# Reordering the loads and the first products of a fused spectral-mixer and MLP block, forward and backward

## The chip, the cores and the metric

The kernel runs on one core of a Trainium2 chip. The metric is the device time of one execution in microseconds (us). Five engines of a core appear below, each with its own in-order queue of instructions: TensorE (PE, matrix products; PEld is its loading of weights), VectorE (DVE), ScalarE (ACT), GpSimd (POOL) and SyncE (SP), which here does little but issue DMA transfers. "PEq", "SPq" and so on are the queues where an issue itself is recorded.

## The reference

The program computes a block and all of its gradients. S = 2048 tokens, D = 1024, F = 3584, bfloat16 in and out:

```python
mod = (silu(c) @ w_mod).reshape(1, 6, 1, -1)
sa, ca, ga, sb, cb, gb = mod rows 0..5
h = layernorm(x) * (1 + ca) + sa
x = x + ga * irfft2(rfft2(h) * (w_r + 1j * w_i))
h = layernorm(x) * (1 + cb) + sb
x = x + gb * (gelu(layernorm(h) @ w1 + b1) @ w2 + b2)
```

The outputs are x and, by `jax.vjp` with `grad_out`, the nine gradients for x, w_r, w_i, w1, b1, w2, b2, c and w_mod.

## The kernel before, in words

The Fourier transforms are products with tables of sines and cosines, after "folds" that use the symmetries of tokens and columns. The tokens lie in four chunks of 512; a chunk is loaded half in plain order by SP and half in turned order by indirect DMAs of POOL (`load_tok`, L142). F is worked in 28 blocks of 128 rows ("blocks" below).

The tile framework lays the instructions of each engine in an order by its own priorities, following the order of the code except where `issue_after` or `high_priority` says otherwise. What stands in an engine's queue runs in that order.

The stages that matter here, in the order of the program:

1. **Lead-in** (to about 60 us). The rows ca and gb of `mod` are made by `mod_block` (L273): for each half row eight products of silu(c) with a 128x8x512 block of w_mod (tile `wblk`, 1 MB, a ring of three slots), a cast, and for ca an addition of 1 on DVE. Chunks 0 and 1 of x get their layer norm: chunk 0 on DVE (`ln_dve`, L391), chunk 1 on ACT (`ln_act`, L376: four passes for sums, four for squares). `norm_act` (L417) applies the norm, DVE multiplies by the row 1 + ca. The gb row is turned into a column (tile `pc`, L434).
   grad_out comes in four quarters of 512 tokens (`load_go`, L350, 1 MB each). Each quarter is turned by 32 products with an identity or a reversing matrix (tile `pt`, L466); DVE (L470) and ACT (L474) evacuate the turned quarter and scale it by gb into `gBoT`. Then g·w2^T for the quarter and the first two blocks: sixteen products (`ph_part`, tile `pp`, L450). A block is 32 products; its four results are cast by DVE or ACT (L456), and POOL stores the block to `d_ph` in memory. w2^T comes through transposing DMAs on SP (`load_w2t`, L341; `wt` has four slots).
   POOL and DVE make indices for the sine tables, ACT the sines (L527). The sa row follows (L849), its first half and its second straight behind the last quarter.
2. **Blocks ahead of the spectral part.** `PH_EARLY = 8` (L868): blocks 0 to 7, and block 8 behind the loop, so nine of the 28 blocks lead. While PE works on them, DVE and ACT norm chunks 2 and 3 and fold the tokens.
3. **Spectral part** (from 120.18 us): `s_fwd` (tile `pu`, L573), the products with W, and the way back; its last products (tile `po`) end at 219.30 us. Behind it PE does the blocks that are left (L943); DVE and ACT at the same time consume the transform's output chunk by chunk (`consume_fwd`, L898): unfold, multiply by ga, add x, a layer norm (`ln_mix`, L401: half on DVE, half on ACT L410 and L413; `norm_act` L421), multiply and add cb and sb, a second norm. The normed chunk 0 is turned into `n3Ta` among the last blocks (L957).
4. **First MLP product.** A list by hand (`plan`, L1096) gives PE's order: z(0,0), the second halves of the four last blocks (64 products), z(0,1) to z(0,3), then first and second product in turn. z(b,g) is 32 products of token quarter b and four columns of w1 (L1006), evacuated by ACT (L1009) from two pools of two slots (`ps_s`, `ps_d`); the gelu and its derivative follow on ACT (L1013, L1017, L1019) and DVE. `bo` is the second product (L1060).

Behind that come the gradients. A third pool, `ps_f`, has four slots for the results of the blocks; before the change the turned quarters of grad_out use it too.

Of the kernel before, what the change touches and what calls it, by code (L numbers as in the profile page):

```python
# [10 lines left out]
FP32 = mybir.dt.float32  # L11
BF16 = mybir.dt.bfloat16
# [23 lines left out]
def kernel(  # L36
# [407 lines left out]
    def ph_part(fc, js, behind_=None):  # L444
        ph2 = phs[fc % 4]
        for j in js:
            pp = ps_f("pp")
            for cch in range(NDC):
                with tc.issue_after(behind_.ins) if behind_ else ExitStack():
                    last_pe[0] = nc.tensor.matmul(pp[:], lhsT=wt[:, fc % 4, cch, :], rhs=gBoT[j][:, cch, :],  # L450
                                                  start=(cch == 0), stop=(cch == NDC - 1))
            q = (0, 2, 3, 1)[j]
            ov = ph2[:, :, q * P:(q + 1) * P]
            pv = pp[:, :].rearrange("p (i w) -> p i w", w=P)
            with tc.high_priority():
                nc.any.tensor_copy(out=ov, in_=pv)  # L456
        if js[-1] == 3:
            nc.gpsimd.dma_start(out=d_ph[fc * P:(fc + 1) * P, :], in_=ph2.rearrange("p i w -> p (i w)"))

    for j in range(4):  # L460
        for cch in range(NDC):
            pt = ps_f("pt")
            for a in range(4):
                q = (0, 2, 3, 1)[a] if j % 2 == 0 else (1, 3, 2, 0)[a]
                with ordered() if last_pe[0] else ExitStack():
                    last_pt = nc.tensor.matmul(pt[:, q * P:(q + 1) * P], lhsT=gos[j][:, a, cch * P:(cch + 1) * P], rhs=(ident, irev)[a // 2],  # L466
                                               start=True, stop=True)
            if cch % 2 == 0:
                with tc.high_priority():
                    nc.vector.tensor_scalar(out=gBoT[j][:, cch, :], in0=pt[:], scalar1=gb_col[:, cch:cch + 1], scalar2=0.0,  # L470
                                            op0=ALU.mult, op1=ALU.add, accum_out=gu[:, j, cch:cch + 1])
            else:
                with tc.high_priority():
                    nc.scalar.activation(out=gBoT[j][:, cch, :], in_=pt[:], func=ACT.Identity, scale=gb_col[:, cch:cch + 1],  # L474
                                         accum_out=gu[:, j, cch:cch + 1])
        for fc in range(2):
            ph_part(fc, (j,), last_pt)

    gslot = [0]

    def gview(width, dt):
        o = gslot[0]
        gslot[0] += (2 * width + 15) // 16 * 16
        return genv[:, o:o + 2 * width].bitcast(dt)

    def iota(pattern, base, mult, width):
        ti = gview(width, I32)
        nc.gpsimd.iota(ti, pattern=pattern, base=base, channel_multiplier=mult)
        return ti

    def to_f(ti, width):
        tf = gview(width, FP32)
        nc.gpsimd.tensor_copy(out=tf, in_=ti)
        return tf

    def pts(out, in0, s1, s2, o0, o1=None):
        kw = {} if o1 is None else {"op1": o1}
        nc.gpsimd.tensor_scalar(out=out, in0=in0, scalar1=s1, scalar2=s2, op0=o0, **kw)

    kevi = iota([[1, 264]], 0, 0, 264)  # L500
    kevc = kevi.bitcast(FP32)
    nc.gpsimd.tensor_copy(out=kevc, in_=kevi)
    kev = gview(512, FP32)
    for r in range(2):
        pts(kev[:, r * 256:(r + 1) * 256], kevc[:, 0:256], 2.0, float(r), ALU.mult, ALU.add)
    kod = gview(512, FP32)
    for r, (mul, add) in enumerate(((2.0, 1.0), (-2.0, 1023.0), (2.0, 257.0), (-2.0, 767.0))):
        pts(kod[:, r * P:(r + 1) * P], kevc[:, 0:P], mul, add, ALU.mult, ALU.add)
    rown = to_f(iota([[256, 2]], 1, 2, 2), 2)
    rowr = to_f(iota([[-256, 2]], 1023, -2, 2), 2)  # L510
    rowo = [(rown, rowr)[r % 2][:, r // 2:r // 2 + 1] for r in range(4)]
    rowe = [rown[:, r:r + 1] for r in range(2)]
    jf, jod = kevc, kod.rearrange("p (s w) -> p s w", w=256)[:, :, 0:P]
    gidx = reg.tile([P, 2, 1024], I32, name="gidx", tag="px0")
    gcount, trig_in = [0], [None]

    def trig(dst, colv, rowv, nrow, width, modn, cosine):
        idx = gidx[:, gcount[0] % 2, :]
        gcount[0] += 1
        sh = float(3 * modn // 4 if cosine else modn // 2)  # L520
        for r in range(nrow):
            ov = idx[:, r * width:(r + 1) * width]
            pts(ov.rearrange("p (s w) -> p s w", s=2) if len(colv.shape) == 3 else ov, colv, rowv[r], sh, ALU.mult, ALU.add)
        n = nrow * width
        nc.vector.tensor_scalar(out=idx[:, 0:n], in0=idx[:, 0:n], scalar1=modn - 1, scalar2=None, op0=ALU.bitwise_and)
        with tc.issue_after(x_sqrt.ins):
            trig_in[0] = nc.scalar.activation(out=dst, in_=idx[:, 0:n].rearrange("p (r w) -> p r w", w=width), func=ACT.Sin,  # L527
                                 bias=negpi[:], scale=2 * np.pi / modn)
# [5 lines left out]
    def gen_mats():  # L534
        for cl, colv, modn in ((CE, kev, 2048), (SE, kev, 2048), (CO, kod, 4096), (SO, kod, 4096)):
            sm = (smA, smB)[cl % 2]
            rows, n = (rowo, 4) if cl % 2 else (rowe, 2)
            if cl == SE:
                nc.gpsimd.memset(kev[:, 0:1], 512.0)
            for r in range(0, n, 2):  # L540
                trig(sm[:, cl // 2, r:r + 2, :], colv, rows[r:r + 2], 2, 512, modn, cl < 2)
            if n == 2:
                nc.gpsimd.dma_start(out=d_SF[:, cl, 0:n], in_=sm[:, cl // 2])
        for cl, colv, modn in ((CE, jf[:, 0:256], 1024), (SE, jf[:, 1:257], 1024), (CO, jod, 2048), (SO, jod, 2048)):
            trig(em1[:, 0, 2 * cl:2 * cl + 2, :], colv, rowe, 2, 256, modn, cl < 2)
# [308 lines left out]
    gb2s = small.tile([P, NDC], FP32, tag="u_rt", bufs=1)  # L854
    nc.vector.reduce_sum(out=gb2s[:], in_=gu[:, 0:4, :].rearrange("p j c -> p c j"), axis=AX.X)
# [872 lines left out]
```

## Time and profile before

| | us |
|---|---|
| median of 3 runs | 1386.9 (1386.55 to 1392.74) |
| span of the profiled execution | 1385.4 |
| PE busy / DVE busy / ACT busy | 1357.9 / 1067.4 / 765.1 |
| first product of the spectral part | 120.18 |
| first product of z(0,0) / z(0,4) | 316.24 / 361.57 |

The profiled execution's span runs from its first to its last instruction; the median lies 1.5 us above it, which is taken as what lies around the span. In the rows quoted below a timeline gives the start, the duration, the engine, the line and operation, output and input, shapes, the count, and in brackets the idle time of the engine just ahead of it with what ended that. A row of a table by windows gives the busy time of PE, PEld, DVE, ACT and POOL (in brackets the instructions), then the granted clock of PE as a share of full speed, the busy share of the 16 DMA engines and GB/s.

### The profile page before, as it was taken

The page shows a single profiled execution, that of the slowest core. Times are in us where ns is not written, and L with a number is a line of the kernel's source. Part 1 is how long each engine was busy: PE and PEld are TensorE (multiplying, and loading weights), DVE is VectorE, ACT ScalarE, POOL GpSimd, SP SyncE. Part 2 cuts the span into 40 slices and gives each one's busy share as a digit, 9 for nine tenths or more (in the row PEclk, how much of TensorE's full clock was granted, in tenths as well). Part 3 has the DMA queues.
Part 4 walks back from the last instruction along what each step waited for, and adds up shares of the span by engine and source line. Part 5 has one row for each costly group of instructions (what it writes and reads, how often), then busy time and mean ns, then how long its engine had stood idle before and what let it go on. Part 6 is the DMA issues. An engine that isn't in the chain of part 4 may idle for free. (4 is left out here: it accounts for less than half of the span.)

```text
span 1385.4 us, 18669 instructions
## 1 busy us (share of the span) xinstructions
PE 1357.9 (98%) x6931; PEld 655.6 (47%) x6931; DVE 1067.4 (77%) x1477; ACT 765.1 (55%) x1084; POOL 357.4 (26%) x438
## 2 busy tenths in 40 slices
PE   5899999999999999999999999999999999999999
PEld 2445565444443444444444444444654555454444
DVE  5898889997988787887711488889888588968980
ACT  6855667658877765765413684446633464544311
POOL 5340633201112122122211011112344320332351
PEclk9999999999999999999999999999999999999999
DMA  9973665999787776697899779998779879899991
GB/s 329 279 243 88 166 173 179 258 272 362 252 258 228 223 253 223 205 279 252 256 309 220 210 187 275 293 294 243 205 217 264 223 150 263 214 252 244 308 329 52
DMA packets 356177, 330.08 MB, mean 238 GB/s; under 512 B 203834, under 2 KB 298448, under 8 KB 355958
## 3 DMA queue, kind: packets, MB, share of 16 engines
q1 hardware_dynamic: 313990, 200.76, 56.1%
q0 software_dynamic: 35328, 120.26, 25.5%
q10 hardware_dynamic: 6768, 7.87, 1.6%
q8 instruction: 54, 0.88, 0.3%
q14 instruction: 37, 0.30, 0.1%
HBM read 165.73 MB, written 114.87 MB: 203 GB/s over the span
## 5 line engine op out<-in xcount | busy, mean ns | idle before, releaser
L450 PE MATMUL pp<-gBoT,wt 128*128 128x512 bf16 x896 | 200.2, 381 | 0.5 <-DVE gBoT L470 0.3
L1160 PE MATMUL pg<-w1T,gzr 128*128 128x512 bf16 x896 | 196.0, 379 | 0.8 <-DMA gzr<-d_gz 0.8
L1596 PE MATMUL gw1acc<-gzh,n3n 128*128 128x512 bf16 x640 | 139.6, 379 | 0.0
L1006 PEld LDWEIGHTS <-w 128*128 128x128 bf16 x896 | 87.4, 98 | 108.5 <-issue 4.4
L1160 PEld LDWEIGHTS <-gzr 128*128 128x128 bf16 x896 | 86.5, 98 | 109.6 <-issue 5.9
L1596 PEld LDWEIGHTS <-n3n 128*128 128x128 bf16 x896 | 87.4, 98 | 105.2 <-issue 1.3
L450 PEld LDWEIGHTS <-wt 128*128 128x128 bf16 x896 | 87.6, 98 | 102.5 <-issue 3.1
L1006 PE MATMUL pz<-n3Tb,w 128*128 128x512 bf16 x448 | 100.1, 382 | 2.3 <-DVE w2sD L1082 2.3
L1006 PE MATMUL pz<-n3Ta,w 128*128 128x512 bf16 x448 | 98.7, 379 | 0.0
L1009 ACT ACTIVATE gt<-pz,b_col 128x512 bf16<-128x512 f32 x112 | 73.3, 683 | 41.0 <-PE pz L1006 40.6
L195 DVE TENSOR_TENSOR ct<-ct 128x2048 bf16<-128x2048 bf16 (+1 forms) x84 | 91.5, 1118 | 5.1 <-ACT n L421 2.5
L1600 ACT CAST gwo<-gw1acc 128x512 bf16<-128x512 f32 x56 | 32.3, 582 | 111.5 <-PE gw1acc L1596 85.8
L1060 PEld LDWEIGHTS <-hhA 128*128 128x128 bf16 x608 | 59.0, 98 | 72.0 <-issue 1.8
L1332 PE MATMUL gw2acc<-gB,hhsA 128*128 128x512 bf16 x416 | 92.4, 379 | 0.0
L1017 ACT ACTIVATE gt<-gt 128x2048 bf16<-128x2048 bf16 x28 | 53.5, 1910 | 55.4 <-DVE gt L195 55.3
L195 DVE TENSOR_TENSOR gt<-gt,gt 128x2048 bf16<-128x2048 bf16 x56 | 68.5, 1224 | 18.1 <-ACT gt L1019 16.9
L1340 ACT CAST gwo<-gw2acc 128x512 bf16<-128x512 f32 x40 | 23.6, 589 | 87.4 <-PE gw2acc L1332 87.4
L1332 PEld LDWEIGHTS <-hhsA 128*128 128x128 bf16 x416 | 40.7, 98 | 47.2
L1596 PE MATMUL gw1acc<-gzu,n3n 128*128 128x512 bf16 x256 | 55.4, 379 | 0.0
L1013 ACT ACTIVATE gt<-gt 128x2048 bf16<-128x2048 bf16 x28 | 53.4, 1909 | 3.5 <-DVE hhC L195 2.8
L1019 ACT ACTIVATE gt<-gt 128x2048 bf16<-128x2048 bf16 x28 | 53.4, 1907 | 0.4
L1332 PE MATMUL gw2acc<-gB,otl 128*128 128x512 bf16 x224 | 50.0, 379 | 0.0
(380 smaller groups left out, 2528.6 us busy)
## 6 DMA issues: line engine op xcount, KB each, us to landing
gzr<-d_gz SPq DMA_DIRECT2D x28, 512.0 KB
wblk<-in_w_mod_dram SPq DMA_DIRECT2D x12, 1024.0 KB
d_ph<-pho POOLq DMA_DIRECT2D x21, 512.0 KB, 5.4
out_dram<-otl POOLq DMA_DIRECT2D x40, 256.0 KB, 4.4
d_hh<-hhA POOLq DMA_DIRECT2D x19, 512.0 KB, 5.5
wrw<-in_w_mod_dram SPq DMA_DIRECT2D x32, 256.0 KB
out_dram<-gwo POOLq DMA_DIRECT2D x57, 128.0 KB, 4.4
w<-in_B_w_dram SPq DMA_DIRECT2D x7, 1024.0 KB
```

What stands on the lines that cost most here:

```text
L195: return nc.vector.tensor_tensor(out=out, in0=a, in1=b, op=op)
L450: last_pe[0] = nc.tensor.matmul(pp[:], lhsT=wt[:, fc % 4, cch, :], rhs=gBoT[j][:, cch, :], start=(cch == 0), stop=(cch == NDC - 1))
L1006: last_pe[0] = nc.tensor.matmul(pz[:], lhsT=w1s[g][:, cch, k * P:(k + 1) * P], rhs=n3T[:, cch, :], start=(cch == 0), stop=(cch == NDC - 1))
L1009: z_in = nc.scalar.activation(out=zb[:, k, :], in_=pz[:], func=ACT.Identity, bias=b1_col[:, fc:fc + 1], scale=1.0)
L1013: nc.scalar.activation(out=av, in_=zb, func=ACT.Square)
L1017: nc.scalar.activation(out=sg, in_=bv, func=ACT.Sigmoid, scale=2.0 * GK)
L1019: nc.scalar.activation(out=bv, in_=bv, func=ACT.Sigmoid, scale=-2.0 * GK)
L1060: last_pe[0] = nc.tensor.matmul(pbs[i][:], lhsT=hh[:, k, i * P:(i + 1) * P], rhs=wp[:, k, :], start=False, stop=(g == 6 and k == 3))
L1160: last_pg[0] = nc.tensor.matmul(pgs[i][:], lhsT=gzs[b, g][:, k, i * P:(i + 1) * P], rhs=w1Ts[g][:, k, h * KH:(h + 1) * KH], start=(g == 0 ...
L1332: nc.tensor.matmul(acc[:], lhsT=hh_of(fc)[:, t, :], rhs=gBs[t // 4][:, t % 4, h * KH:(h + 1) * KH], start=(t == 0), stop=(t == NT - 1))
L1596: nc.tensor.matmul(acc[:], lhsT=n3ns[t // 4][:, t % 4, cch * P:(cch + 1) * P], rhs=gz2[t // 8][:, t % 8, :], start=(t == 0), stop=(t == NT ...
L1600: w1g["ev"] = nc.scalar.copy(out=ob, in_=acc[:])
```

## The change

Seven edits, all of order:

- SP issues the two halves of the gb row ahead of everything, then quarter 0 of grad_out, and the x chunks between the later quarters; the ca row comes after the last quarter (first half) and behind two w2^T transposes (second half).
- The turned halves of x chunks 0 and 1 are issued by POOL behind the first index tables (`load_x_turned`).
- Quarter 0 is turned by itself; the turns of quarter j+1 then stand among the sixteen products of quarter j, at the places `TURN_AT`.
- The turned quarters use the pools `ps_s` and `ps_d` (two slots each; even columns go to DVE, odd to ACT) instead of `ps_f`.
- The products for the ca row follow the last quarter; `small_rows` (the gradient of b2 and b1's column) moves into the loop of blocks.
- `PH_EARLY` is 10 instead of 8: eleven blocks lead the spectral part, and two fewer follow it.
- Index making (`trig_idx`) is separated from the sines (`trig_sin`).

The number of instructions on PE stays at 13857. The first `pu` product stands 64 products later in PE's queue than before; the first `pn` and the first z(0,0) product stand at the same place of the queue in both.

In the pieces of queues that follow, the number ahead of a row is its place in the queue; where numbers are skipped, rows are left out. SP's queue at the start of the program, before (`x_0` is x chunk 0, `go` and `fbuf` are quarters of grad_out, `wblk` blocks of w_mod in the order ca, gb, sa, ga):

```order
2 L144 DMA x_0_138<-in_A_x_dram 128x2x1024
3 L271 DMA wblk<-in_w_mod_dram 128x8x512
4 L144 DMA x_1_139<-in_A_x_dram 128x2x1024
5 L271 DMA wblk<-in_w_mod_dram 128x8x512 x3
6 L351 DMA go_143<-in_grad_out_dram 128x4x1024
7 L342 DMA_TRANSPOSE wt<-in_B_w_dram 128x8x128 x2
8 L351 DMA go_144<-in_grad_out_dram 128x4x1024
9 L351 DMA fbuf<-in_grad_out_dram 128x4x1024 x2
10 L342 DMA_TRANSPOSE wt<-in_B_w_dram 128x8x128 x2
13 L271 DMA wblk<-in_w_mod_dram 128x8x512 x3
14 L342 DMA_TRANSPOSE wt<-in_B_w_dram 128x8x128 x2
```

The same queue of the changed kernel, where the order of the `wblk` blocks is gb, ca, sa, ga:

```order
2 L271 DMA wblk<-in_w_mod_dram 128x8x512 x2
3 L351 DMA go_143<-in_grad_out_dram 128x4x1024
4 L342 DMA_TRANSPOSE wt<-in_B_w_dram 128x8x128 x2
6 L434 DMA x_0_138<-in_A_x_dram 128x2x1024
8 L434 DMA x_1_139<-in_A_x_dram 128x2x1024
10 L271 DMA wblk<-in_w_mod_dram 128x8x512
12 L271 DMA wblk<-in_w_mod_dram 128x8x512
13 L144 DMA x_2_140<-in_A_x_dram 128x2x1024
15 L271 DMA wblk<-in_w_mod_dram 128x8x512
16 L342 DMA_TRANSPOSE wt<-in_B_w_dram 128x8x128 x2
17 L271 DMA wblk<-in_w_mod_dram 128x8x512 x4
```

Row 15 is the first half of the sa row and row 17 begins with its second: the two transposes of row 16, for blocks 4 and 5, which stood behind sa and the first half of ga, stand between the halves now.

ACT's queue in the lead-in, before (`x_1` passes are the norm of chunk 1, `gBoT_133` to `gBoT_136` the evacuations of the turned quarters 0 to 3):

```order
3 L379 ACTIVATE fbuf,sv<-x_1_139 128x1024 x2
4 L282 CAST rows_87<-pm 128x512
5 L379 ACTIVATE fbuf,sv<-x_1_139 128x1024 x2
6 L382 ACTIVATE fbuf,sv<-x_1_139,sv 128x1024 x4
10 L474 ACTIVATE gBoT_133,gu<-pt,gb_col 128x512 x4
```

And of the changed kernel:

```order
4 L553 ACTIVATE gBoT_133,gu<-pt,gb_col 128x512 x4
5 L458 ACTIVATE fbuf,sv<-x_1_139 128x1024
6 L553 ACTIVATE gBoT_134,gu<-pt,gb_col 128x512
7 L458 ACTIVATE fbuf,sv<-x_1_139 128x1024
8 L553 ACTIVATE gBoT_134,gu<-pt,gb_col 128x512 x2
10 L553 ACTIVATE gBoT_134,gu<-pt,gb_col 128x512
11 L458 ACTIVATE fbuf,sv<-x_1_139 128x1024 x2
```

The passes over chunk 1 stood ahead of every evacuation; now they stand among the evacuations of quarters 1 to 3.

ACT's queue at the first z blocks, before (`gt` tiles take the evacuations of z; the `x4` of L1009 in row 154 are z(0,1), in row 156 z(0,2)):

```order
148 L456 CAST pho<-pp 128x4x128
149 L1017 ACT_TABLE_LOAD
150 L1017 ACTIVATE gt_3114<-gt_3114 128x2048
151 L421 ACTIVATE ct<-xt,stats 128x1024 x4
152 L1019 ACTIVATE gt_3114<-gt_3114 128x2048
153 L456 CAST phr<-pp 128x4x128
154 L1009 ACTIVATE gt_3260<-pz,b_col 128x512 x4
155 L1013 ACTIVATE gt_3260<-gt_3260 128x2048
156 L1009 ACTIVATE gt_3113<-pz,b_col 128x512 x4
```

And of the changed kernel, where L1054 is the evacuation of z, L500 the norm pass, L1058, L1062 and L1064 the former L1013, L1017 and L1019:

```order
147 L500 ACTIVATE ct<-xt,stats 128x1024
148 L1054 ACTIVATE gt_3260<-pz,b_col 128x512
149 L500 ACTIVATE ct<-xt,stats 128x1024
150 L1054 ACTIVATE gt_3260<-pz,b_col 128x512
154 L1054 ACTIVATE gt_3260<-pz,b_col 128x512
155 L1062 ACT_TABLE_LOAD
156 L1062 ACTIVATE gt_3114<-gt_3114 128x2048
157 L1058 ACTIVATE gt_3260<-gt_3260 128x2048
158 L1064 ACTIVATE gt_3114<-gt_3114 128x2048
159 L1054 ACTIVATE gt_3113<-pz,b_col 128x512 x4
```

The norm passes of chunk 3 now alternate with the evacuations of z(0,1), and the table load and three gelu passes stand between these and the evacuations of z(0,2) (row 159); before, the gelu passes of z(0,0) stood ahead of z(0,1)'s evacuations.

The diff, cut to its core:

```diff
-    load_tok(x4s[0], A_x, 0)
-    mod_get(1, 0)
-    load_tok(x4s[1], A_x, 1)
-    mod_get(1, 1)
-    mod_get(5, 0)
-    for h in range(2):
-        mod_block(1, h, wm[1, h][:])
-    mod_get(5, 1)
-    load_go(0)
-    load_w2t(0)
-    load_w2t(1)
-    for j in range(1, 4):
-        load_go(j)
-    for h in range(2):
-        mod_block(5, h, wm[5, h][:])
-    load_w2t(2)
-    load_w2t(3)
...
+    first_idx = [token_idx(k) for k in range(2)]
+    for h in range(2):
+        mod_get(5, h)
+    load_go(0)
+    load_w2t(0)
+    load_w2t(1)
+    load_go(1)
...
+    load_x_plain(0)
+    load_go(2)
+    load_x_plain(1)
+    for i in range(2):
+        load_x_turned(i)
+    load_go(3)
+    mod_get(1, 0)
+    load_w2t(2)
+    load_w2t(3)
+    for h in range(2):
+        mod_block(5, h, wm[5, h][:])
+    mod_get(1, 1)
...
-            pt = ps_f("pt")
+        pt = (ps_s, ps_d)[cch % 2]("pt")
...
+    TURN_AT = (4, 5, 7, 8, 10, 11, 13, 14)
+    for cch in range(NDC):
+        turn_go(0, cch)
+    for j in range(4):
+        n = 0
+        for fc in range(2):
+            pp = ps_f("pp")
+            for cch in range(NDC):
+                if j < 3 and n in TURN_AT:
+                    turn_go(j + 1, TURN_AT.index(n))
+                n += 1
+                with ordered():
+                    last_pe[0] = nc.tensor.matmul(pp[:], lhsT=wt[:, fc, cch, :], rhs=gBoT[j][:, cch, :],
+                                                  start=(cch == 0), stop=(cch == NDC - 1))
+            ph_out(fc, j, pp)
+    for h in range(2):
+        with ordered():
+            mod_block(1, h, wm[1, h][:])
...
-    PH_EARLY = 8
+    PH_EARLY = 10
     for fc in range(PH_EARLY):
         if fc > 1:
             ph_part(fc, (0, 1, 2, 3))
         load_w2t(fc + 4)
+        if fc == 4:
+            with ordered():
+                small_rows()
```

More of the change, by code (lines that the diff above doesn't have):

```diff
@@ new lines, in to_f, with pts @@
+    def to_f(ti, width):
+        tf = gview(width, FP32)
+        nc.gpsimd.tensor_copy(out=tf, in_=ti)
+        return tf
+    def pts(out, in0, s1, s2, o0, o1=None):
+        kw = {} if o1 is None else {"op1": o1}
+        pool_in[0] = nc.gpsimd.tensor_scalar(out=out, in0=in0, scalar1=s1, scalar2=s2, op0=o0, **kw)
+    kevi = iota([[1, 264]], 0, 0, 264)
+    kevc = kevi.bitcast(FP32)
+    nc.gpsimd.tensor_copy(out=kevc, in_=kevi)
+    kev = gview(512, FP32)
+    for r in range(2):
+        pts(kev[:, r * 256:(r + 1) * 256], kevc[:, 0:256], 2.0, float(r), ALU.mult, ALU.add)
@@ new lines, in trig_sin, with token_idx @@
+    def trig_sin(dst, made):
+        with tc.issue_after(x_sqrt.ins):
+            trig_in[0] = nc.scalar.activation(out=dst, in_=made[0], func=ACT.Sin, bias=negpi[:], scale=2 * np.pi / made[1])
+    token_mats = []
+    for cl, colv, modn in ((CE, kev, 2048), (SE, kev, 2048), (CO, kod, 4096), (SO, kod, 4096)):
+        rows, n = (rowo, 4) if cl % 2 else (rowe, 2)
+        token_mats += [(cl, r, n, (colv, rows[r:r + 2], 2, 512, modn, cl < 2)) for r in range(0, n, 2)]
+    def token_idx(k):
+        cl, _, _, args = token_mats[k]
+        if cl == SE:
+            nc.gpsimd.memset(kev[:, 0:1], 512.0)
+        return trig_idx(*args)
@@ L457, in ph_part @@
[L457 to L461, printed above, removed]
-            pt = ps_f("pt")
[L463 to L528, printed above, removed]
+                last_pe[0] = nc.tensor.matmul(pp[:], lhsT=wt[:, fc % 4, cch, :], rhs=gBoT[j][:, cch, :],
+                                              start=(cch == 0), stop=(cch == NDC - 1))
```

99 lines of the change are left out of this document (74 added, 25 removed).

## The prediction

> **What bounds the kernel now.** I read the page first, then the waits of TensorE (PE), then PE's, ScalarE's (ACT) and VectorE's (DVE) timelines in the two stretches that the change touches.
>
> ```profile
> span 1385.4 us, 18669 instructions
> PE 1357.9 (98%) x6931; PEld 655.6 (47%) x6931; DVE 1067.4 (77%) x1477; ACT 765.1 (55%) x1084; POOL 357.4 (26%) x438
> ```
>
> PE is busy in 1357.9 of 1385.4 us: the program is a line of products, and only its 27.5 us of gaps can be won. The waits (line, releaser: total, times, longest) say where:
>
> ```profile
> PE pm L279 <- DMA wblk<-in_w_mod_dram: 9.2, 3, 5.6
> PE pt L466 <- DVE gBoT L470: 2.5, 4, 1.8
> PE ptc L205 <- DMA genv<-in_c_dram: 2.3, 1, 2.3
> PE pt L466 <- ACT gBoT L474: 1.7, 3, 1.1
> PE ptr L210 <- DVE gb_bf L857: 1.3, 1, 1.3
> ```
>
> All of these lie in the first 70 us: PE waits for the first blocks of w_mod, then for evacuations of turned grad_out. The windows show the lead-in as a whole, and its end on the DMA side (column after PEclk):
>
> ```profile
> 0.00:59.70 59.70, 41.10 (x250) 20.64 (x251) 40.65 (x99) 41.98 (x74) 26.36 (x58) 0.97 1.01 306
> 52.00:54.00 2.00, 2.00 (x7) 0.63 (x6) 2.00 (x7) 2.00 (x6) 0.67 (x1) 0.50 1.07 366
> 54.00:56.00 2.00, 2.00 (x10) 0.92 (x9) 1.30 (x3) 0.51 (x1) 1.72 (x4) 0.96 0.37 118
> ```
>
> Until 59.7 PE works 41.1 us and idles 18.6, while the DMA share is 1.01: the engines of the DMA have no free time until about 54.7. So the order of the loads decides what PE can do, and the last load that PE needs there decides when it ends.
>
> **The change, part by part.** *The lead-in.* PE's timeline (start, duration):
>
> ```profile
> 8.03 3.57 PE L279 MATMUL pm<-wblk,u_b 128*128 128x512 bf16 x8 [5.57 <-DMA wblk<-in_w_mod_dram]
> 28.62 3.61 PE L450 MATMUL pp<-gBoT,wt 128*128 128x512 bf16 x16
> 49.55 0.27 PE L466 MATMUL pt<-ident,fbuf 128*128 128x128 bf16 x2 [1.76 <-DVE gBoT L470]
> 51.47 4.92 PE L450 MATMUL pp<-gBoT,wt 128*128 128x512 bf16 x16
> 56.23 3.62 PE L279 MATMUL pm<-wblk,u_b 128*128 128x512 bf16 x16
> 59.68 2.54 PE L450 MATMUL pp<-gBoT,wt 128*128 128x512 bf16 x11
> ```
>
> A product takes 3.61/16 = 0.22 us at full clock. Before, everything of the lead-in ends at 59.68. Afterwards the gb row is first in the queue: its first half no longer has 0.5 MB of x ahead of it, at some 0.37 MB/us 1.4 us less, so PE starts near 6.5. Up to the last grad_out quarter PE has 41.1 - 3.6 (sa row) - about 4.5 (ca row, now behind: sixteen products at 0.22 to 0.45) = 33 us of work, ending near 39.5; I add 3 us for turns that wait (below): 42.5. Then ca, both halves, at full clock 3.5, sa's first half 1.8, ten products of block 2 2.2: PE stands at sa's second half at 50.0.
>
> When is that half there? SP's timeline of its issues:
>
> ```profile
> 27.60 10.91 SPq L342 DMA_TRANSPOSE wt<-in_B_w_dram  x2
> 39.74 6.54 SPq L271 DMA_DIRECT2D wblk<-in_w_mod_dram  x3
> 54.70 3.49 SPq L342 DMA_TRANSPOSE wt<-in_B_w_dram  x2
> ```
>
> Before, sa's halves and ga's first went out in one go, 39.74 to 46.28, sa's second about 43.9. The transfers end at 54.7 with ga's 1 MB, 2.9 us at 366 GB/s, so sa's second had landed near 51.8, 8 us after its issue. Afterwards two w2^T transposes stand ahead of it on SP, and they wait for the products that free their slots, the last quarter's (42.5). With their 3.5 us of issuing, sa's second half goes out at 46.0 (its own slot, one of three, is free when the first ca half is used, at 44.3) and lands at 54.0. PE idles 4.0 there.
>
> Such a pause costs clock: after the 1.76 us pause at 49.55 the sixteen products took 4.92 instead of 3.61, 1.3 us more, at the 0.50 that the window 52 to 54 shows. I take 3.57 for the eight products (the row at 8.03, half clock): done at 57.6. Before, the same work including the ten products ends at 59.68 + 2.2 = 61.9. That is 4.3 us won; the 1.3 us wait for gb_bf goes too (its small rows move among later products), half of which I count: **front gain 5**.
>
> The Trainium skill, "TensorE: Matmul & The Clock Gate", Part 1, says the clock halves after an idle window of about 3.4 us and that these windows run freely. The trace halves it after 1.76 us of pause with sparse turns on either side, so the measurement decides; by the rule a pause under 3.4 us would often cost nothing, and the gain would be some 1 us more.
>
> Bounds of the gain: not more than if sa's second half lands at 51.8 and PE runs warm, 61.9 - 53.5 + 1.3 = 9.7; not less than if the transposes hold SP the 10.9 us of the row at 27.60: issue at 53.4, landing near 60 as the queue is empty by then, products done at 63.5, gain -1.
>
> Turns that wait. ACT's passes over x chunk 1 ran before any turn was due:
>
> ```profile
> 9.40 1.06 ACT L379 ACTIVATE fbuf<-x 128x1024 bf16<-128x1024 bf16 x1 [6.50 <-DMA x<-in_A_x_dram]
> 19.01 1.15 ACT L382 ACTIVATE fbuf<-x,sv 128x1024 bf16<-128x1024 bf16 x1 [3.50 <-DVE sv L380]
> ```
>
> Now the eight passes, 8.8 us in all, stand between its evacuations of quarters 1 to 3, the first two of them until the turned half of the chunk has landed; and each engine evacuates from two slots of its own instead of four in common. Behind a waiting pass are ACT's four evacuations of quarter 1, and PE waits for those. My 3 us for it lie between nothing (the chunk lands early, the products cover the passes) and the 8.8. The price is PE time before 50.0, and PE has 4.0 us to spare there: up to 7 us of it cost nothing, 8.8 would cost 1.8.
>
> *Cover of the DVE at the spectral start.*
>
> ```profile
> 39.15 2.29 DVE L195 TENSOR_TENSOR fbuf<-fbuf,rows 128x4096 bf16<-128x4096 bf16 x1 [0.96 <-ACT fbuf L421]
> 117.67 0.69 DVE L195 TENSOR_TENSOR fbuf<-fbuf,sb_saf 128x1024 bf16<-128x1024 bf16 x1
> 120.18 1.04 PE L573 MATMUL pu<-smA,fbuf 128*128 128x256 bf16 x8
> ```
>
> The ca row is there at 46 + cast and add, 47: the multiplication moves 8 us, the fold ends at the latest at 118.4 + 8 = 126.4. PE arrives at 120.18 + 64 x 0.2157 (13.8) - 5 = 129.0. Nothing waits; the cover is 2.6 us.
>
> *Two blocks less behind the spectral part.* They are 13.8 us of PE under which DVE and ACT consumed the transform's output (two norms per chunk). That work starts 13.8 - 5 = 8.8 later on the clock, while the first z block comes 5 earlier. Who is late? The first MLP stage:
>
> ```profile
> 323.15 13.98 PE L450 MATMUL pp<-gBoT,wt 128*128 128x512 bf16 x64
> 336.96 20.88 PE L1006 MATMUL pz<-n3Ta,w 128*128 128x512 bf16 x96
> 361.57 7.07 PE L1006 MATMUL pz<-n3Ta,w 128*128 128x512 bf16 x32
> 318.54 0.15 DVE L195 TENSOR_TENSOR stats<-mv,stats 128x4 f32<-128x4 f32 x1
> 331.68 0.15 DVE L195 TENSOR_TENSOR stats<-mv,stats 128x4 f32<-128x4 f32 x1
> 318.78 4.64 ACT L421 ACTIVATE ct<-ct,stats 128x1024 bf16<-128x1024 bf16 x4 [0.59 <-DVE stats L195]
> 325.03 1.15 ACT L413 ACTIVATE ct<-xt,mv 128x1024 bf16<-128x1024 bf16 x1
> 327.86 1.91 ACT L1013 ACTIVATE gt<-gt 128x2048 bf16<-128x2048 bf16 x1
> 329.66 0.30 ACT L386 ACTIVATE mv<-mv,eps_c 128x4 f32<-128x4 f32 x1
> 330.45 1.28 ACT L1017 ACT_TABLE_LOAD   x1
> 331.79 1.91 ACT L1017 ACTIVATE gt<-gt 128x2048 bf16<-128x2048 bf16 x1
> 358.66 2.40 ACT L1009 ACTIVATE gt<-pz,b_col 128x512 bf16<-128x512 f32 x4
> 320.25 0.69 DVE L456 CAST phr<-pp 128x512 bf16<-128x512 f32 x1
> ```
>
> Eight casts leave with the blocks; half of them on DVE at 0.6 each give the chain 2.4 back (ends: none, 4.8). The chain is 8.8 - 2.4 = 6.4 late: the statistics of chunk 2 at 318.54 come at 324.9. ACT then runs, in its new order: four norm passes 4.6, one sum pass 1.2, two square passes 2.5, one square of gt 1.9, root 0.3, to 335.5; chunk 3's statistics at 336.0; four pairs of norm pass and z evacuation, 4 x (1.16 + 0.6) = 7.0, to 343.0; table 1.28, two passes of L1017 and L1019 and one of L1013, 5.7, to 350.0; the first evacuation of z(0,2) ends at 350.7. PE wants that slot for z(0,3) at 336.96 + 2 x 6.96 - 5 = 345.9. It waits 4.8 and pays 1.3 of clock: **6.1 given back**.
>
> Bounds:
>
> ```profile
> 320.00:340.00 20.00, 20.00 (x95) 9.04 (x94) 10.39 (x18) 19.92 (x23) 2.35 (x4) 1.00 1.06 378
> 340.00:362.00 22.00, 22.00 (x106) 9.80 (x104) 21.64 (x29) 16.43 (x19) 5.57 (x5) 1.00 0.88 263
> ```
>
> DVE has 9.6 us free in the first window and ACT 5.6 in the second: nothing is given back if these take it all. If nothing gives, the slack of z(0,3)'s evacuation before 361.57 is 361.57 - 359.33 = 2.2, and 13.8 - 2.2 = 11.6 is lost, with the clock 12.9. ACT's 19.92 of 20.00 speaks for a value in the middle.
>
> *Edits at nothing:* the index tables earlier on POOL, x turned by POOL behind them, the d_ph stores ahead of the table's store. Only the norm of x and the fold wait for these, and the fold has its 2.6 us of cover; beyond that a late x costs PE time one for one. The small rows at block 4 put two short products among long ones. Behind z(0,4) PE's order is unchanged.
>
> **Sum.** -5 + 6.1 = +1.1. Span 1385.4 to 1386.5; 1.5 us lie around the span (median 1386.9), so 1388.0. A measurement can tell about 0.5% (6.9 us) from no change.
>
> **Rivals.** *Gain kept* (0.22): DVE's 9.6 and ACT's 5.6 us of idle take the delay. For: they are there. Against: ACT has none between 320 and 340, where the norms and the z evacuations meet. Gives 1386.9 - 5 = 1382, at the upper front gain 1377.
>
> *Chain rigid* (0.15, slower): ACT at the first z blocks swallows none of the 13.8 us of lost cover beyond 2.2; z(0,3) or z(0,4) waits 11.6 plus 1.3, less 5: +7.9, 1394.8. It is slower by over 0.5% from a wait of 10.6 on. For: ACT's 19.92. Against: idle after 340.
>
> *Late sa row* (0.20): the transposes on SP hold it, front gain between -1 and 1, while the giving back stays 6.1: 1392 to 1394.1. For: 10.91 us for two transposes at 27.60. Against: 3.49 at 54.70, with the queue emptier.
>
> **How the numbers follow.** The forecast (0.43) is 1388, its own range 1384 to 1392 (gain 3 to 7, giving back 4 to 8). Faster takes two thirds of the gain-kept case, 0.15; slower all of the rigid chain and a quarter of the late row, 0.20; the rest, 0.65, is within 0.5%. The range, 1379.5 to 1395, leaves out the deep end of the kept gain and a rigid chain on a late row, under 2 in 10.
>
> **What would show it.** PE's wait for wblk before the second sa half, 3 to 5 us with half clock behind it; the first pu product at 128 to 130, not waiting for DVE; a PE wait on ACT's evacuation at z(0,2) or z(0,3) of 4 to 6 us; z(0,4) within 2 us of 361.57. I am wrong if no wait stands at the first z blocks, if sa's second half is there before PE, or if pu waits for the fold.

## The result, and the profile after

The changed kernel is slower: 1401.7 us (median of 4 runs) against 1389.8 for the kernel before on the same chips, a ratio of 1.0091 with a 95% interval of 1.0068 to 1.0113. (The 1386.9 ahead of the prediction is the median of three of the four runs behind the 1389.8.) Forecast were 1388.0 us and no change that can be told. The profiled execution's span is 1397.7 us, 12.3 more than before.

PE's waits in the changed kernel (L279 is still the w_mod blocks, L546 the turns, L537 the products of the blocks, L1051 the z products):

```profile
PE pm L279 <- DMA wblk<-in_w_mod_dram: 9.5, 3, 5.4
PE pp L537 <- ACT pho L529: 4.8, 2, 4.3
PE pt L546 <- ACT gBoT L553: 4.0, 4, 2.2
PE pp L537 <- DMA wt<-in_B_w_dram: 3.6, 1, 3.6
PE pz L1051 <- ACT gt L1054: 2.6, 2, 2.1
PE pt L546 <- DMA go<-in_grad_out_dram: 2.4, 2, 1.6
PE pp L537 <- DVE pho L529: 1.4, 1, 1.4
PE pt L546 <- DVE gBoT L550: 1.1, 2, 0.7
```

The waits that the change was to shorten did not fall: w_mod 9.5 (9.2 before), evacuations of turned quarters 5.1 (4.2 before), a quarter's load 2.4 (0.5 before). New are waits for casts of the blocks' results (`pho`, on ACT and DVE), for a w2^T tile from the DMA (`wt`), and for z's evacuations. PE's timeline of the changed kernel shows where each stands (start, duration, the idle time ahead in brackets):

```profile
56.26 3.60 PE L279 MATMUL pm<-wblk,u_b 128*128 128x512 bf16 x8 [5.41 <-DMA wblk<-in_w_mod_dram]
59.65 12.64 PE L537 MATMUL pp<-gBoT,wt 128*128 128x512 bf16 x54
...
86.01 3.61 PE L537 MATMUL pp<-gBoT,wt 128*128 128x512 bf16 x16 [1.37 <-DVE pho L529]
90.15 3.61 PE L537 MATMUL pp<-gBoT,wt 128*128 128x512 bf16 x16 [0.53 <-ACT pho L529]
...
130.84 9.79 PE L537 MATMUL pp<-gBoT,wt 128*128 128x512 bf16 x32 [4.27 <-ACT pho L529]
140.48 1.04 PE L613 MATMUL pu<-smA,fbuf 128*128 128x256 bf16 x8
...
319.39 8.77 PE L537 MATMUL pp<-gBoT,wt 128*128 128x512 bf16 x32 [3.56 <-DMA wt<-in_B_w_dram]
327.99 7.07 PE L1051 MATMUL pz<-n3Ta,w 128*128 128x512 bf16 x32
...
364.76 8.75 PE L1051 MATMUL pz<-n3Ta,w 128*128 128x512 bf16 x32 [2.07 <-ACT gt L1054]
...
377.94 7.07 PE L1051 MATMUL pz<-n3Ta,w 128*128 128x512 bf16 x32 [0.54 <-ACT gt L1054]
```

And one place of the kernel before that the change did away with:

```profile
439.10 2.86 PE L1006 MATMUL pz<-n3Tb,w 128*128 128x512 bf16 x8 [2.25 <-DVE w2sD L1082]
441.75 4.37 PE L1060 MATMUL pbo<-w2sC,hhC 128*128 128x512 bf16 x16
```

Read at the same instruction in both timelines, the change's lag is this:

| up to | before | after | lag | what happened on the way |
|---|---|---|---|---|
| sa row and ten products of block 2 | 59.68 + 2.16 = 61.84 | 59.65 | -2.2 | the lead-in is shorter |
| first pu product | 120.18 + 13.80 (64 products) | 140.48 | +6.5 | casts waited for: 1.37, 0.53, 4.27; half clock behind the last (0.50 granted from 130.90 to 135.00): 9.79 instead of 7.07 for 32 products, 0.9 behind 59.65; the 1.3 for gb_bf gone |
| z(0,0) | 316.24 | 327.99 | +11.8 | w2^T tile 3.56, half clock 8.77 instead of 7.07 |
| z(0,4) | 361.57 | 377.94 | +16.4 | z evacuations 2.07 and 0.54, half clock 8.75 instead of 7.07 |
| end | 1385.4 | 1397.7 | +12.3 | the wait of 2.25 at 439.10 and its half clock, 1.7, not there |

The wait of 2.25 is not gone for good with the order of the loads: with eight blocks ahead (below) the changed kernel has it again, 3.50 at 447.61.

The largest single loss is the one at 130.84. ACT's timeline says what its cast waited for, POOL's what held that up, and DVE's what ran meanwhile:

```profile
130.21 2.05 ACT L529 CAST pho<-pp 128x512 bf16<-128x512 f32 x4 [9.92 <-DMA d_ph<-pho]
```

```profile
95.79 25.66 POOL L633 DMA_INDIRECT ws<-in_A_w_r_dram,xu  x1 [2.80 <-PE pm L279]
...
124.08 0.95 POOL L633 DMA_INDIRECT ws<-in_A_w_r_dram,xu  x1 [0.31 <-issue]
...
126.29 1.17 POOL L531 DMA_DIRECT2D d_ph<-pho  x2
```

```profile
94.45 2.27 DVE L195 TENSOR_TENSOR fbuf<-fbuf,rows 128x4096 bf16<-128x4096 bf16 x1
...
102.33 0.27 DVE L284 TENSOR_SCALAR rows<-rows 128x512 bf16<-128x512 bf16 x1
...
119.30 1.21 DVE L195 TENSOR_TENSOR x<-fbuf 128x2048 bf16<-128x2048 bf16 x1
120.44 0.15 DVE L1228 CAST u_rt<-u_bfc 128x8 f32<-128x8 bf16 x1
...
130.30 0.69 DVE L195 TENSOR_TENSOR fbuf<-fbuf,sb_saf 128x1024 bf16<-128x1024 bf16 x1
```

The cast of block 9 needs the slot of block 5 in `pho`, and that slot is free once POOL's store of block 5 has landed. That store is one of the two at 126.29. Ahead of it in POOL's queue stands an indirect load of W, 25.66 us long, and those 25.66 us are a stretch in which DVE has no gap at all:

```profile
95.00:121.00 26.00, 26.00 (x122) 11.72 (x120) 26.00 (x28) 11.81 (x20) 25.21 (x1) 1.00 0.24 52
```

DVE is busy 26.00 of 26.00, POOL 25.21 with one instruction, and the DMA engines are busy 0.24 of the time, at 52 GB/s, so it is not for want of free DMA engines that the load waits. It ends at 121.45, one us after a small cast with a single input (120.44). Up to there DVE ran sums of two inputs one behind the other, but for two additions of a constant, 0.27 us each (the row at 102.33 and one at 103.73), at which the load did not come through. In the kernel before the same load stands earlier and is shorter, and with nine blocks ahead nobody waits for the slot:

```profile
70.34 6.13 POOL L593 DMA_INDIRECT ws<-in_A_w_r_dram,xu  x1 [0.31 <-PE pp L450]
```

### The profile page after: what moved, and what is told of

It reads as the page before. It is cut to its first block, busy times and chain, and to the rows that moved or that the text cites. A ratio compares the mean times of both kernels' runs of the same rounds, so it can differ in the third digit from the quotient of the medians.

```text
span 1397.7 us, 18662 instructions
## 1 busy us (share of the span) xinstructions
PE 1360.1 (97%) x6931; PEld 655.8 (47%) x6931; DVE 1069.4 (77%) x1479; ACT 763.4 (55%) x1082; POOL 380.0 (27%) x438
## 4 chain that ended last, share of the span: by engine, by line
PE 74%; DVE 4%; ACT 3%; DMA 2%; issue 1%; DVEq 0%; ACTq 0%
PE pg L1205 14%; PE gw2acc L1377 14%; PE gw1acc L1641 14%; PE pbo L1105 11%; PE pz L1051 9%; PE pp L537 6%; DVE gt L195 2%; PE po L845 2%; DMA wt<-in_B_w_dram 1%; PE pcs L652 1%; PE pu L1521 1%; DMA w2sA<-in_B_w_dram 1%; ACT gt L1062 1%; ACT gt L1054 1%; ACT gt L1064 1%
## 5 line engine op out<-in xcount | busy, mean ns | idle before, releaser
L537 PE MATMUL pp<-gBoT,wt 128*128 128x512 bf16 x832 | 190.2, 386 | 9.7 <-ACT pho L529 4.8
L1051 PEld LDWEIGHTS <-w 128*128 128x128 bf16 x896 | 87.7, 98 | 110.3 <-issue 7.2
L537 PEld LDWEIGHTS <-wt 128*128 128x128 bf16 x832 | 82.3, 99 | 108.2 <-issue 14.6
L1051 PE MATMUL pz<-n3Ta,w 128*128 128x512 bf16 x448 | 100.5, 384 | 2.6 <-ACT gt L1054 2.6
L1051 PE MATMUL pz<-n3Tb,w 128*128 128x512 bf16 x448 | 99.2, 379 | 0.2 <-DVE w2sD L1127 0.2
L1054 ACT ACTIVATE gt<-pz,b_col 128x512 bf16<-128x512 f32 x112 | 72.2, 684 | 37.2 <-PE pz L1051 37.0
L1062 ACT ACTIVATE gt<-gt 128x2048 bf16<-128x2048 bf16 x28 | 53.5, 1911 | 56.3 <-DVE gt L195 56.3
L529 ACT CAST pho<-pp 128x512 bf16<-128x512 f32 x55 | 31.1, 585 | 49.3 <-PE pp L537 39.3
L1058 ACT ACTIVATE gt<-gt 128x2048 bf16<-128x2048 bf16 x28 | 53.4, 1907 | 5.1 <-DVE w2sA L195 2.3
L1064 ACT ACTIVATE gt<-gt 128x2048 bf16<-128x2048 bf16 x28 | 53.4, 1909 | 0.5
```

The source lines that it names most:

```text
L1051: last_pe[0] = nc.tensor.matmul(pz[:], lhsT=w1s[g][:, cch, k * P:(k + 1) * P], rhs=n3T[:, cch, :], start=(cch == 0), stop=(cch == NDC - 1))
L1054: z_in = nc.scalar.activation(out=zb[:, k, :], in_=pz[:], func=ACT.Identity, bias=b1_col[:, fc:fc + 1], scale=1.0)
L1058: nc.scalar.activation(out=av, in_=zb, func=ACT.Square)
L1062: nc.scalar.activation(out=sg, in_=bv, func=ACT.Sigmoid, scale=2.0 * GK)
L1064: nc.scalar.activation(out=bv, in_=bv, func=ACT.Sigmoid, scale=-2.0 * GK)
```

## The experiments

The numbers of a run are those of its profiled execution, the ratio is that of its timed runs to the kernel before on the same chip, with the 95% interval. The profiled execution is one of the timed runs and lies up to 4.0 us from their median, and the timed runs of one version differ by 4 to 20 us. So a span alone does not tell two versions apart that lie a few us from each other: the places in a profile tell what happened in that execution, the ratio tells what it is worth. Theories: **stores** (POOL's blocked queue costs what is lost ahead of the spectral part), **cover** (two blocks less behind it cost the rest), against **fold** (the ca row at the end makes DVE's fold late, and the two blocks only hide that).

**Eight instead of ten blocks ahead.**

```diff
-    PH_EARLY = 10
+    PH_EARLY = 8
```

> The changed kernel with PH_EARLY back at 8: nine blocks lead the spectral part, all else as changed. Theory (two blocks less behind the spectral part, and POOL's queue ahead of it, cost the time; the front itself wins): the first pu product 13.8 us earlier than in the changed kernel and 7.0 more without the wait for the cast, at about 119.5; no wait for w2^T near 319 and none for z's evacuations; span about 1384. Rival (the fold on DVE ends 12.6 us later than before because the ca row comes last, and two more blocks only hide it): pu waits for DVE until about 131, span about 1396.

Span 1394.4, ratio 1.0062 (1.0040 to 1.0084). PE's timeline:

```profile
119.92 0.38 PE L613 MATMUL pu<-smA,fbuf 128*128 128x256 bf16 x2
120.14 5.99 PE L537 MATMUL pp<-gBoT,wt 128*128 128x512 bf16 x27
131.45 1.46 PE L613 MATMUL pu<-smA,fbuf 128*128 128x256 bf16 x6 [5.32 <-DVE fbuf L195]
```

The rival was right in the main: the first two pu products stand at 119.92, as the theory had it, and the rest wait for the fold until 131.45. Before, the fold ended at 118.4; in the changed kernel at 131.0 (the row at 130.30). The front that the change wins is useless alone, because the spectral part has two conditions and the change made the other one 12.6 us late. Why late, DVE's queue of the changed kernel says:

```profile
61.97 0.69 DVE L529 CAST pho<-pp 128x512 bf16<-128x512 f32 x1 [7.18 <-PE pp L537]
69.19 2.28 DVE L195 TENSOR_TENSOR fbuf<-fbuf,rows 128x4096 bf16<-128x4096 bf16 x1
```

A cast of block 2 stands ahead of the fold and waits 7.18 us for PE, which itself waits for the sa row (56.26); the first multiplication by the ca row, at 39.15 before, is at 69.19.

**Ten blocks ahead in the kernel before.**

```diff
-    PH_EARLY = 8
+    PH_EARLY = 10
```

> The kernel before with PH_EARLY 10 instead of 8, nothing else. Theory: POOL had its W loads behind it at 85 us there, so no cast waits ahead of the spectral part and pu starts at 120.2 + 13.8 = 134.0; the two blocks less behind it cost about 5.3 (a w2^T tile comes late, and the clock) and 4.6 (evacuations of z), of which 4 come back at later waits: span about 1391. Rival (nothing is lost behind the spectral part by the missing blocks alone): 1385.

Span 1393.2, ratio 1.0043 (1.0010 to 1.0076); pu at 134.6 without a wait.

```profile
314.89 8.77 PE L450 MATMUL pp<-gBoT,wt 128*128 128x512 bf16 x32 [4.96 <-DMA wt<-in_B_w_dram]
...
360.26 7.07 PE L1006 MATMUL pz<-n3Ta,w 128*128 128x512 bf16 x32 [2.06 <-ACT gt L1009]
...
373.44 7.07 PE L1006 MATMUL pz<-n3Ta,w 128*128 128x512 bf16 x32 [2.24 <-ACT gt L1009]
```

Cover is shown by itself: the late w2^T tile (4.96 and half clock) and the waits for z's evacuations come with the number alone, in the old order of loads. The price was 7.8, some 2 more than expected. The fold does not matter here, since PE arrives after it.

**W's first loads on POOL behind the store of block 8.**

```diff
-                nc.gpsimd.indirect_dma_start(out=ws[:, x, 1 - sl, 0:DF], out_offset=None, in_=w, in_offset=w_idx(par, m))
+                with tc.issue_after(ph_in[8].ins) if fwd and n < 2 else ExitStack():
+                    nc.gpsimd.indirect_dma_start(out=ws[:, x, 1 - sl, 0:DF], out_offset=None, in_=w, in_offset=w_idx(par, m))
```

> The changed kernel with POOL's first four loads of W placed behind its store of block 8. Theory: the stores of blocks 5 to 8 no longer wait behind these loads, block 9's casts find free slots, the 4.27 us wait and the 2.7 us of half clock go: pu at about 133.5, span about 1390.7. Rival (the casts wait for something else, or the W loads come too late for the first pair): pu stays at 140, span 1397 or more.

Span 1396.6, ratio 1.0029 (0.9990 to 1.0068). POOL and PE:

```profile
99.14 0.56 POOL L533 DMA_DIRECT2D d_ph<-pho  x1 [5.63 <-ACT pho L531]
107.28 0.53 POOL L533 DMA_DIRECT2D d_ph<-pho  x1 [7.58 <-ACT pho L531]
...
121.95 1.26 POOL L636 DMA_INDIRECT ws<-in_A_w_r_dram,xu  x1 [0.33 <-PE pp L539]
```

```profile
133.83 1.04 PE L615 MATMUL pu<-smA,fbuf 128*128 128x256 bf16 x8
...
315.28 8.65 PE L539 MATMUL pp<-gBoT,wt 128*128 128x512 bf16 x32 [6.17 <-DMA wt<-in_B_w_dram]
```

Stores holds up to pu, which starts at 133.83, 6.7 earlier, without a wait on a cast. The gain did not reach the end of this execution: the w2^T tile was waited for 6.17 instead of 3.56, and later waits grew, so 1.1 us are left in the profile, which lies 3.9 us above the median of this version's runs. The span's expectation failed; the interval of the timed runs ends where the changed kernel's begins and leaves more. The plain stores, 0.56 and 0.53 us each, went through in the very stretch in which the indirect load had been held up.

**Pauses in DVE's fold.** Four statistics instructions with one input, 0.67 us each, between the fold's sums:

```diff
+            made = part()
+            if i > 1:
+                with tc.issue_after(made.ins):
+                    nc.vector.bn_stats(out=pause[:], in_=opca_row[:, 0:512])
```

> The changed kernel with four short statistics instructions (0.65 us each, one input) between the fold's two-input sums on DVE; their results are not used. Theory (POOL's first load of W takes 25.66 us because DVE's two-input sums follow one another without a gap and keep POOL from its memory port): that load ends within 2 us of the first pause, at about 101 instead of 121.4, the stores of blocks 5 to 8 leave from 105 on, the 4.27 us wait ahead of the spectral part goes, pu at about 134. Rival (the load waits for free places in its DMA queue, or for data): it still ends near 121 and pu stays at 140.

Span 1399.8, ratio 1.0106 (1.0056 to 1.0155). DVE's pauses and POOL's loads:

```profile
99.28 0.67 DVE L936 BATCH_NORM_STATS2 pause<-rows 128x6 f32<-128x512 bf16 x1
...
112.37 0.67 DVE L936 BATCH_NORM_STATS2 pause<-rows 128x6 f32<-128x512 bf16 x1
...
119.71 0.67 DVE L936 BATCH_NORM_STATS2 pause<-rows 128x6 f32<-128x512 bf16 x1
```

```profile
96.16 4.13 POOL L633 DMA_INDIRECT ws<-in_A_w_r_dram,xu  x1 [2.80 <-PE pm L279]
100.60 12.70 POOL L633 DMA_INDIRECT ws<-in_A_w_i_dram,xu  x1 [0.31 <-issue]
113.61 7.00 POOL L633 DMA_INDIRECT ws<-in_A_w_r_dram,xu  x1 [0.30 <-issue]
120.91 2.57 POOL L633 DMA_INDIRECT ws<-in_A_w_i_dram,xu  x1 [0.30 <-issue]
```

Three of the four loads end about one us after a pause has begun: 100.29 after the one at 99.28, 113.30 after 112.37, 120.61 after 119.71; the fourth ends at 123.48, after a small cast at 122.57. What holds such a load is DVE's unbroken row of sums, then, and not its data or a full queue, which a pause on DVE would not bring. But sums do not hold every load: the one at 124.08 in the changed kernel took 0.95 us while DVE ran two sums from 122.95 to 125.33. What makes that difference stays open. The Trainium skill, "SBUF — State Buffer", Who interferes with whom, says that a DVE instruction with two SBUF inputs contends with a POOL instruction that reads SBUF, and not with one that only writes. The traces agree in part: the indirect load takes its row numbers from a table there (`xu`) and was held 25.66 us, the plain stores passed in 0.53, but the load at 124.08 passed among such sums. pu came at 134.3 as expected. The expectation failed on the stores, though, which left at 123.5 and not at 105, because the second and third load needed a pause each; and the w2^T tile, now 7.57 late, took the gain.

**The w2^T tile: w1's loads behind it**, in the kernel before with ten:

```diff
-            load_w1({24: 1, 25: 1, 27: 5}.get(fc, 0))
+            load_w1({27: 7}.get(fc, 0))
```

> The kernel before with PH_EARLY 10 and all seven loads of w1 behind the last w2^T transposes on SP; before, two of these 1 MB loads stand ahead of them. Theory (the late w2^T tile, 4.96 us plus clock, comes from transposes that queue behind other transfers, w1's among them): the wait shrinks to below 1.5 us, z(0,0) 5 us earlier, at about 318, some of it given back at the evacuations of z; span 1388 to 1390. Rival (the transposes meet the stores of the consumed chunks, not w1): wait unchanged, span 1393.

Span 1393.4, ratio 1.0026 (1.0006 to 1.0045).

```profile
312.74 3.63 PE L450 MATMUL pp<-gBoT,wt 128*128 128x512 bf16 x16 [0.96 <-DMA wt<-in_B_w_dram]
...
366.82 7.07 PE L1006 MATMUL pz<-n3Ta,w 128*128 128x512 bf16 x32 [2.23 <-ACT gt L1009]
```

The wait fell from 4.96 to 0.96 and z(0,4) came 6.6 us earlier than in the run without this edit (373.44); 1.6 of these stood already at pu (133.07 against 134.63), which the edit does not touch. Two 1 MB loads ahead of the last transposes on SP make the tile late, then, when there are 13.8 us less to fetch it in. They are not all of it: of the five runs with ten blocks ahead and this order four had a late tile, and the one with the sa row late (below) had none. The profiled span does not show it, since a wait of 3.0 us for ACT stands at 888 in this execution (below).

The same edit in the changed kernel:

> The changed kernel with all loads of w1 behind the last w2^T transposes on SP, nothing else. Theory (w1's loads hold the last w2^T tile back here as in the kernel before with ten): the 3.56 us wait at 319 and its 1.7 us of half clock go, z(0,0) at about 322.7, pu still at 140.5; of the 5.3 us won some 3 remain at the end, the rest goes into other waits: span 1393 to 1396. Rival (transposes held by other transfers): wait unchanged, span 1397.7.

The wait for the tile is gone, z(0,0) is at 319.96 and z(0,4) at 371.70, 6.2 earlier; 2.5 of these stood already at pu (137.99), which the edit does not touch. Ratio 1.0046 (1.0020 to 1.0072) against the changed kernel's 1.0091. The profiled span, 1397.5, has a wait far behind that the changed kernel's profile does not have:

```profile
894.35 11.34 PE L1205 MATMUL pg<-w1T,gzr 128*128 128x512 bf16 x44 [4.12 <-ACT gn3a L1221]
```

Such a wait, 1.9 to 4.1 us, stood in five of the profiles (W late, pauses, both runs with this edit alone, and the last one below) and not in the others. What brings it was not tried.

**The sa row used behind block 3.**

```diff
-        with ordered():
-            mod_block(0, h, wm[0, h][:])
...
+        if fc == 3:
+            sa_rows()
```

> The changed kernel with both halves of the sa row used behind block 3 instead of ahead of and within block 2. Theory (PE and, behind it, DVE stand still for that load): the 5.41 us wait at 50.8 and its half clock go, DVE's fold ends up to 7 us earlier, POOL's W loads come free earlier with it, pu 7 to 8 us earlier, span about 1390. Rival (the lead-in is bound by the DMA engines, so the wait comes back at the next w2^T tile): span 1396 to 1398.

Span 1387.5, ratio 1.0018 (0.9986 to 1.0050).

```profile
123.35 8.34 PE L537 MATMUL pp<-gBoT,wt 128*128 128x512 bf16 x32 [2.88 <-ACT pho L529]
131.53 1.04 PE L613 MATMUL pu<-smA,fbuf 128*128 128x256 bf16 x8
...
365.63 7.07 PE L1056 MATMUL pz<-n3Ta,w 128*128 128x512 bf16 x32 [2.24 <-ACT gt L1059]
```

pu came 9.0 earlier; the fold ended at 124.1 instead of 131.0, since DVE's cast no longer stood still, and POOL's long load, still 24.78 us, ended at 114.58 instead of 121.45. 10.2 us of span for the place of sixteen products: the wait for that load had cost PE, and through a cast in its queue DVE, and through DVE POOL.

**The old order of loads, quarters turned among products, nine blocks ahead.**

```diff
-            pt = ps_f("pt")
+        pt = (ps_s, ps_d)[cch % 2]("pt")
...
+                if j < 3 and n in TURN_AT:
+                    turn_go(j + 1, TURN_AT.index(n))
...
-    PH_EARLY = 8
+    PH_EARLY = 9
```

> The kernel before with its old order of loads, but with the quarters turned among products in the two pools of two slots, as in the change, and PH_EARLY 9. Theory (the ca row first keeps the fold early, at 118 to 119; the interleaving alone takes away 4 to 5 us of waits for turned quarters; one block more ahead fits between fold and spectral part): lead-in 4 to 5 us shorter, pu at about 122, no wait on DVE there, z(0,4) at 357 to 360, span 1381 to 1384. Rival (the missing block behind costs as much as is won): span 1385 to 1388.

Span 1390.0, ratio 1.0059 (1.0030 to 1.0089): the theory fell. The interleaving shortened the lead-in by 1.3 us (sa's products ended at 58.4) and not by 4 to 5 (PE then waited 2.89 for a turned quarter on DVE and 2.3 for the next quarter's load), and the fold ended at 123.1 although the ca row was early; pu came at 124.24 (expected 122). z(0,4) was at 359.05, in the expected span, but a 3.51 us wait at 441 and others between gave it back.

**sa late, W late, nine blocks.** The two edits of above with the store of block 7:

> The changed kernel with the sa row used behind block 3, the first loads of W on POOL behind the store of block 7, and PH_EARLY 9. Theory (the fold's end, 124 in the run with sa late, is the bound of the spectral part's start, and one block less behind costs little): pu at about 124 with a wait of some 3 us on DVE, no late w2^T tile, z(0,4) near 359, span 1382 to 1385. Rival (the start is not bound by the fold): pu at 120.5.

Span 1382.5, pu waits 3.6 for DVE, z(0,4) at 360.12, no late tile: as expected. The timed runs give 1.0006 (0.9982 to 1.0030), no difference from the kernel before.

**The same with chunk 3's statistics on ACT.**

> The run with sa late, W late and PH_EARLY 9, and besides the norm statistics of x chunk 3 on ACT (eight passes) instead of DVE (8 statistics instructions, 5.2 us). Theory (DVE's own work bounds the fold's end at 123): fold 3 to 5 us earlier, pu at 120 to 121 with hardly a wait on DVE, span about 1380. Rival (ACT's norms or POOL's making of indices hold DVE as much): fold's end within 1 us of 123.6, span 1382 to 1384.

The fold ended at 121.8, 1.8 earlier, less than the theory's 3 to 5; and PE waited 12.31 us for the last w2^T tile, with w1 in its old order and nine blocks ahead, which brought no late tile in the run above. What made it late here was not tried. The span is 1392.5 and the ratio 1.0068 (1.0042 to 1.0095).

**W late and w1 last**, sa as in the change:

> The changed kernel with both: W's first loads on POOL behind the store of block 8, and w1 behind the last w2^T tiles; the sa row as in the change. Theory: pu at 133.8 as in the run with W late, no late w2^T tile, z(0,0) at about 316, z evacuations waited for 4 to 6 us, z(0,4) at 366 to 368, span 1388 to 1390; the run with sa late as well was 1384.1, so sa's place is worth 4 to 6. Rival (sa's place is worth nothing behind the spectral part, since the consume chain is the bound there): span within 1.5 us of 1384.

Span 1387.7, ratio 1.0025 (1.0002 to 1.0047); pu 133.6, z(0,0) 315.53, z(0,4) 367.27: as expected. Two edits take away 10.0 of the 12.3 us between the profiles, and 0.0066 of the ratio's 0.0091, some 9 us, in the timed runs.

**All three edits, ten blocks kept.**

> The changed kernel, PH_EARLY 10 kept, with sa late, the W loads behind the store of block 8, and w1 loaded behind the last w2^T tiles. Theory (with PE's accidents ahead of the spectral part gone, the consume chain on DVE and ACT is the bound of the first z blocks, so the tenth block ahead gains nothing over the run with 9): pu at about 127 without a wait on DVE, PE waits for z evacuations 5 to 6 us, z(0,4) at 360 to 362, span 1382 to 1385. Rival (two blocks ahead are worth more once nothing else waits): z(0,4) at 354 to 357, span 1378 to 1380.

```profile
126.66 1.04 PE L615 MATMUL pu<-smA,fbuf 128*128 128x256 bf16 x8
...
347.56 8.75 PE L1059 MATMUL pz<-n3Ta,w 128*128 128x512 bf16 x32 [3.15 <-ACT gt L1062]
...
360.75 7.07 PE L1059 MATMUL pz<-n3Ta,w 128*128 128x512 bf16 x32 [0.54 <-ACT gt L1062]
```

Span 1384.1; 1383.6 us in the timed runs against 1387.5 before, ratio 0.9965 (0.9943 to 0.9987): the one version that beats both kernels, and by little. PE comes to the spectral part at 126.66 and to z(0,4) at 360.75; with nine blocks it waited for the fold until 123.6 and came to z(0,4) at 360.12. What is won ahead of the spectral part is given back at z's evacuations (3.15, half clock, 0.54), as the theory had it. In all four runs with ten blocks ahead and no late tile (sa late, w1 last in the changed kernel, and the last two) z(0,4) stands 233.7 to 234.1 us behind pu, where 241.4 - 13.8 = 227.6 would do without waits. PE waits there in the main for evacuations by ACT; that DVE and ACT set this distance is read from these waits, as no run changed their work there.

## Why the prediction was wrong

*What bounds the kernel, and the lead-in.* Right in kind: the last load that PE needs decides. sa's second half was waited for 5.41 us (forecast 4.0), its eight products took 3.60 at half clock (forecast 3.57), the lead-in with ten products ended at 59.65 (forecast 57.6). The load was issued nearly as forecast (46.45, forecast 46.0) and was there 9.8 us later instead of 8. The front gain of 5 was 2.2 there and 3.5 with the wait for gb_bf, and it did not come from shorter waits: up to the end of these products PE idles 20.0 us (18.6 before) and is busy 39.6 (43.2 before).

*"The fold ends at the latest at 118.4 + 8 = 126.4."* Wrong: 131.0. I moved the fold by the 8 us of the ca row and overlooked what stood ahead of it in DVE's queue, a cast that waits for products behind sa's load. The bound was none. That pu did not wait for the fold all the same, as forecast, was luck: PE came 11.5 us late itself, and at the forecast 129.0 it would have met a fold that ends at 131.0.

*"Edits at nothing: ... Only the norm of x and the fold wait for these."* This is the step that failed. PE came to the spectral part at 140.5 and not at 129.0. No term had the slots of `pho`: four of them, each free only when its store has landed, and the store is in POOL's queue behind loads that the change does not touch. With nine blocks ahead that queue was never waited for; the tenth and eleventh block made it the bound. Runs that let the stores through brought pu to 133.6 to 134.3. What is left to 129.0 is in the main the lead-in, 2.1 longer than forecast, and the casts waited for at 86.01 and 90.15, 1.9.

*A term that was missing altogether* is the w2^T tile, 5.3 us with its half clock. I weighed the cover of DVE and ACT behind the spectral part and not that of the DMA. The two losses do not simply add up: where the stores alone were let through, the tile was waited for 6.17 and 7.57 us instead of 3.56, and the profiles end 1.1 earlier with W late, 0.2 with w1 last, 10.0 with both. How the loss divides between the two is not settled by that, since the timed ratios (1.0029, 1.0046 and 1.0025, against 1.0091) give each alone more than its profile does.

*The giving back at z.* The mechanism was right: 4.6 in the changed kernel (forecast 6.1), the most of it at z(0,3) as forecast. There the late tile had already held PE back. In the four runs with ten blocks ahead and no late tile z(0,4) stands 51.7 us behind z(0,0), against 45.3 before: 6.4 given back, so the size was right too, though the wait at z(0,3) was 3.1 and not 4.8 and shorter ones beside it made up the rest. None of the three signs of being wrong showed: none of them looks at POOL's queue or at the tile. What failed are two of the places forecast, pu at 140.5 (128 to 130) and z(0,4) at 377.9 (361.6). Of the rivals none was the one: the rigid chain gave the time, 1394.8, nearest to the result, by another way.

## What to carry to other kernels

When work is moved ahead of a stage, count the slots that its results occupy, and for each the instruction that frees it, with all that stands ahead of that instruction in its queue. A stage that waits for two engines gains nothing from one of them alone; moving a block of cover takes it away from every engine and transfer that used it, the DMA too. And an instruction that waits in a queue is a wait for all that stands behind it there: PE's wait for one load became DVE's late fold and POOL's late stores.

## What the runs showed of the hardware

An indirect load on POOL took 25.66 us where it was issued among two-input sums that DVE ran without a gap. It lost at the end of some twenty of them and at two additions of a constant (128x512, 0.27 us). It came through about one us after a small cast began (128x8, 0.15 us), in other runs after a statistics instruction of 0.67, and after an operation with a constant on 128x2 numbers (0.15 us at 113.58, the load's end at 114.58 with sa late). Issued one us behind such a small cast it took 1.26 (W late). Why it did not come in between two sums, when the load at 124.08 did, stays open. Plain stores from the same queue took 0.53 us in the same stretch.

The clock fell to a half behind waits of 2.07 us (z(0,3) in the changed kernel, 8.75 instead of 7.07) and 2.06 (z(0,3) with the pauses, 8.75), and behind another of 2.06 it did not (the run with ten blocks before, 360.26: 7.07 for 32 products), so what a pause costs cannot be told from its length.
